# Linear attention into a GELU MLP on one core: batch 2's q in two halves round k, its v cast on GpSimd, and batch 3's k mapped at other blocks

## The chip, the cores and the metric

The kernel runs on one core of a Trainium2 chip. Time is device time in microseconds (us) for one execution. Before the change it is 272.56 us, the median of 6 runs (272.32 to 273.84).

## What is computed

A linear attention with the feature map elu + 1, over 8 batches of 8 heads, 576 positions and 64 values a head, and then a two-layer MLP with a tanh GELU over the 4608 tokens:

```
def phi(x):
    return np.where(x > 0, x, np.exp(x) - 1.0) + 1.0
q_p, k_p = (phi(q), phi(k))
kv = np.einsum('bhsd,bhse->bhde', k_p, v)
z = np.sum(k_p, axis=2)
num = np.einsum('bhsd,bhde->bhse', q_p, kv)
den = np.einsum('bhsd,bhd->bhs', q_p, z)[..., None] + 1e-06
x = (num / den)            # to (4608, 512)
h = x @ w_in               # 512 to 2048
g = 0.5 * h * (1.0 + np.tanh(c * (h + 0.044715 * h * h * h)))
return g @ w_out           # 2048 to 512
```

## The kernel before

The work goes in nine groups. Group j, for j from 0 to 7, takes 512 of the 576 positions of batch j; group 8 takes the 64 positions left over of each batch. For its group, PE (TensorE) makes 16 h blocks (`h_mm`, L391: four matmuls of 128x512 each, then a gelu on ACT at L406), and then the second layer, which from group 1 on is made by seven products (`Products`, L782) of quarters of g and w_out and of their sums and differences, a scheme that saves one product in eight. The sums of w_out are made once (`sum_w_out`, L744, four slices), those of g in each group (L755).

While PE works on group j, the attention of the next batches is prepared in between. The order is written out by hand: `at(j, slot, fn, ...)` registers a piece of work, and `iteration(j)` emits it after step `slot` of group j. In group 1 the steps 0 to 7 are the h blocks 0 to 7, 8 and 9 are products 1 and 7, 10 to 17 are the h blocks 8 to 15, and 18 to 22 are products 2, 6, 5, 4, 3. In groups 2 to 7 the steps 0 to 15 are h blocks, and the products follow. Each engine runs its own instructions strictly in the order in which they are emitted, and waits on semaphores for the others; pieces of one slot come in the order of their registration (`plan_third` first, then `plan_fourth`, and the sums of group 1 last).

For each batch there are these steps:

- q, k and v are loaded in fp32 by SP's DMA queue (L94 and L103) into a pool of seven buffers. Everything up to batch 4's k is issued at the start, as buffers come free.
- The map elu + 1 is the minimum of exp(x) and max(x + 1, 1): `exp_of` on ACT (L221), `linear_of` on DVE (L229) and `least_of` on DVE (L235). The result for k and q is `k_p` and `q_p`. ACT needs one table for exp and another for gelu; a change of table is an ACT_TABLE_LOAD (L419).
- `cast_v` brings v to bf16 (L240, tile `vp`, with a column of ones for the denominator).
- `kv_in_pair` multiplies k_p by vp on PE (L251) in a pair of PSUM banks that kv and n share, and DVE evicts the result (L678 for batch 2, L674 later).
- q_p is transposed by four DMA transposes on SP's queue, one for each of four chunks of 128 positions (`least_q`, L663, tile `qt`).
- n, for each chunk, multiplies qt by kv on PE (L267) and divides by the denominator on DVE (L284, L285, tile `xs`). The chunk is then transposed by SP's queue again into `xt` (L686), the right side of the next group's h blocks. From batch 3 on the n of all chunks is made at one place (L329).

Six PSUM banks of one pool serve the h blocks, the products and the n of some chunks. In group 1, products 1 and 7 keep two of them until the last products, which leaves four for the h blocks 8 to 15.

The change touches two hand-written plans, `plan_third` (batch 2, prepared during group 1) and `plan_fourth` (batch 3, prepared during groups 1 and 2), the helpers `exp_of`, `least_of` and `least_q`, and the slots of two sums in `iteration`. The tile `k_e`, which exp of k writes and `least_of` reads, exists once, so the exp of one batch's k waits for the k minimum of the batch before.

Of the kernel before, what the change touches and what calls it, by code (L numbers as in the profile page):

```python
# [9 lines left out]
BF16 = mybir.dt.bfloat16  # L10
# [6 lines left out]
def kernel(  # L17
# [16 lines left out]
    nc = tc.nc  # L34
# [3 lines left out]
    P = 128  # L38
    HP = P // 2
    C = 4  # L40
    MAIN = P * C
    REST = S - MAIN
    NP = H // 2
# [12 lines left out]
    pt = ctx.enter_context(tc.tile_pool(name="pt", bufs=2))  # L56
# [21 lines left out]
    def bank(name, shape, dt=FP32):  # L78
        return ps_b.tile(shape, dt, name=name, tag="b")
# [120 lines left out]
    def maps_view(name, b, x, out, hs):  # L200


        i = x[:, hs].rearrange("p h (c d) -> p h c d", d=D)
        o = out[:, :, hs, :].rearrange("p c h d -> p h c d")
        if name == "qr" or (name == "q" and b > 1):
            i = i.rearrange("p (u a) c d -> p a u c d", a=2)
            o = o.rearrange("p (a u) c d -> p a u c d", a=2)
        return o, i
# [2 lines left out]
        n, hn = ld[name, b].shape[2] // D, ld[name, b].shape[1]  # L211
        phi[name, b] = pphi.tile([P, n, hn, D], BF16, name=name + "_p")

    def exp_of(name, b, hs=None):
        x = ld[name, b]
        hs = hs or slice(0, x.shape[1])
        if (name, b) not in exps:
            e = name + ("_e" if name != "qr" or b % 2 else "_f")
            exps[name, b] = pe.tile([P, x.shape[2] // D, x.shape[1], D], BF16, name=e)
        o, i = maps_view(name, b, x, exps[name, b], hs)  # L220
        nc.scalar.activation(o, i, AF.Exp)  # L221

    def linear_of(name, b, hs=None):
# [4 lines left out]
        o, i = maps_view(name, b, x, phi[name, b], hs)  # L228
        nc.vector.tensor_scalar(o, i, 1.0, 1.0, op0=ALU.add, op1=ALU.max)  # L229

    def least_of(name, b, hs=None):
        p, e = phi[name, b], exps[name, b]
        if hs:
            p, e = p[:, :, hs, :], e[:, :, hs, :]
        nc.vector.tensor_tensor(p, p, e, op=ALU.min)  # L235


# [149 lines left out]
    xts, qts = {}, {}  # L387

    def h_mm(h_ps, xt, m, ts=slice(0, MAIN), blocks=range(KM)):
        for c in blocks:  # L390
            nc.tensor.matmul(  # L391
                h_ps[:, ts],
                lhsT=w_in_sb[:, c, P * m : P * (m + 1)],
                rhs=xt[:, c, ts],
                start=(c == 0),
                stop=(c == KM - 1),
                skip_group_check=True,
            )

    def gelu(j, g, m, h_ps):  # L400

        g_v, h_v = g[:, :, m, :], h_ps.rearrange("p (a n) -> p a n", a=2)
        if j == B:
            g_v = g[:, :, m, :].rearrange("p a (t n s) -> p (a t) s n", t=2, s=2)
            h_v = h_ps.rearrange("p (t s n) -> p t s n", t=C, s=2)
        nc.scalar.activation(g_v, h_v, AF.Gelu_apprx_tanh)  # L406
# [107 lines left out]
    def at(j, slot, fn, *args):  # L514


        fill.setdefault((j, slot), []).append((fn, args))

    def run(j, slot):
        for fn, args in fill.get((j, slot), ()):  # L520
            fn(*args)
# [70 lines left out]
    def plan_third():  # L592
        def n(c):
            transposed_x(2, c, (nab_in_banks if c == 3 else nab)(qts[2], 2, c))

        at(1, 1, sum_w_out, slice(0, 2))
        at(1, 2, linear_of, "k", 2)
        at(1, 3, linear_of, "q", 2)
        at(1, 4, cast_v, 2)
        at(1, 7, exp_of, "k", 2)  # L600
        at(1, 7, exp_of, "q", 2)
        at(1, 7, gelu_table)
        at(1, 9, least_of, "k", 2)
        at(1, 9, least_q, 2)
        at(1, 12, kv_in_pair, 2)
        for c, slot in enumerate((15, 17, 18, 18)):
            at(1, slot, n, c)

    def plan_fourth():

        at(1, 12, linear_of, "k", 3)
        at(1, 17, exp_of, "k", 3)
        at(1, 18, exp_of, "q", 3)
        at(1, 18, exp_of, "k", 4)
        at(1, 18, gelu_table)
        at(1, 21, linear_of, "q", 3)
        at(1, 22, least_of, "k", 3)
        at(2, 0, cast_v, 3)
        at(2, 0, least_q, 3)
        at(2, 4, kv_in_pair, 3)  # L620
        at(2, 5, linear_of, "k", 4)
        at(2, 5, least_of, "k", 4)
        at(2, 5, cast_v, 4)
        at(2, 8, linear_of, "q", 4)
        at(2, 15, exp_of, "q", 4)
        at(2, 16, exp_of, "k", 5)
        at(2, 19, least_q, 4)
        at(2, 22, linear_of, "k", 5)
        at(3, 0, least_of, "k", 5)
# [26 lines left out]
        at(j, 15, exp_of, "qr", m)  # L656
        at(j, 18, least)

    def least_q(b):
        least_of("q", b)  # L660
        qts[b] = pt.tile([P, C, NP, P], BF16, name="qt")
        for c in range(C):
            nc.sync.dma_start_transpose(  # L663
                out=qts[b][:, c],
                in_=phi["q", b][:, c].rearrange("p h d -> p (h d)"),
            )
# [16 lines left out]
    def transposed_x(b, c, x):  # L683
        if b not in xts:
            xts[b] = pt.tile([P, NP, MAIN], BF16, name="xt")
        nc.sync.dma_start_transpose(out=xt_chunk(b, c), in_=x)  # L686
# [16 lines left out]
    def finish(j, t, o_ps):  # L703
        if t % 2 == 0:
            o_sbs[j, t // 2] = pout.tile([P, 2, d_model], FP32, name="o_sb")
        o_sb = o_sbs[j, t // 2]
        if j == 0 and t in (1, 2):
            at(0, 35, evac, o_sb[:, t % 2, :], o_ps, True)
        else:
            evac(o_sb[:, t % 2, :], o_ps, t < C - 1 if j == 0 else t % 2)  # L710
        if t % 2 == 1:
            ov = out[j * S : j * S + MAIN, :].rearrange("(p c) f -> p c f", c=C)[:, t - 1 : t + 1]

            def store():
                nc.scalar.dma_start(out=ov, in_=o_sb)

            if j == 0:
                at(1, 2, store)
            else:
                store()  # L720

    def o_mm(o_ps, g, t, ms, half=None):
        for m in ms:
            if m == ms.start + 2 and half:
                run(*half)
            nc.tensor.matmul(  # L726
                o_ps,
                lhsT=g[:, t // 2, m, P * (t % 2) : P * (t % 2 + 1)],
                rhs=w_out_sb[:, :, m, :],
                start=(m == 0),  # L730
                stop=(m == MM - 1),
            )
# [139 lines left out]
    def iteration(j):  # L872
        xt = xts[j]
        if j < B:
            g = pg.tile([P, 2, MM, MAIN // 2], FP16, name="g")
        else:
            g = pg.tile([P, MM, 2, MAIN // 2], FP16, name="g").rearrange("p m a n -> p a m n")
        hs = [("h", m) for m in range(MM)]
        us = [range(m, m + 4) for m in range(0, MM, 4)]
        products = Products(j, g) if j else None  # L880
        early, late = slice(0, MM // 4), slice(MM // 4, MM // 2)
        if j == 0:
            us[2:3] = range(8, 10), range(10, 12)
            steps = hs + [("o", t, u) for u in us for t in range(C)]
        elif j == 1:
            steps = hs[:8] + [("product", n) for n in (1, 7)]
            steps += hs[8:] + [("product", n) for n in (2, 6, 5, 4, 3)]
            at(1, 7, products.third_sum, early, False)
            at(1, 7, products.third_sum, late, False)
            at(1, 7, sum_w_out, slice(2, 4))  # L890
            at(1, 13, products.sums, early)
            at(1, 17, products.sums, late)
            at(1, 19, products.last_sum)
        else:
            steps = [hs[i + n] for i in range(MM // 2) for n in (0, MM // 2)]
            steps += [("product", n) for n in (1, 5, 6, 7, 2, 4, 3)]
            for slot, ms in ((7, early), (15, late)):
                at(j, slot, products.sums, ms)
                at(j, slot, products.third_sum, ms)
            at(j, 16, products.last_sum)  # L900
        o_pss = {}
        for slot, step in enumerate(steps):
            if step[0] == "h":
                m = step[1]
                h_ps = h_begun.get(j, {}).get(m)
                if h_ps is None:
                    h_ps = bank("h_ps", [P, MAIN])
                    h_mm(h_ps, xt, m)
                gelu(j, g, m, h_ps)
            elif step[0] == "product":  # L910
                products.step(step[1])
            else:
                t, u = step[1:]
                if u.start == 0:
                    o_pss[t] = bank("o_ps", [P, d_model])
                o_mm(o_pss[t], g, t, u, half=(j, slot - 0.5))
                if u.stop == MM:
                    finish(j, t, o_pss[t])
            run(j, slot)

    plan_second()
    plan_third()
    plan_fourth()
    for j in range(3, 6):
        plan_prepare(j)
# [16 lines left out]
    for j in range(B + 1):  # L942
        iteration(j)
# [30 lines left out]
```

## Time and profile before

| what | value |
|---|---|
| median of 6 runs | 272.56 us |
| the profiled execution: whole time | 272.84 us |
| its span (first to last instruction) | 271.0 us |
| granted TensorE clock | 1.0 throughout |
| group 1's h block 8 begins | 57.93 us |
| group 2's first h block begins | 76.86 us |
| HBM read, written | 36.70 MB, 9.44 MB |

The profile is of one execution. A line of a timeline has start and duration in us, the engine, the line of the code, the operation, what it writes and reads, and the number of instructions merged; in square brackets the engine's idle time before it and what ended that. DVE is VectorE, ACT is ScalarE, POOL is GpSimd, and SPq is the queue of the sync engine, which only issues DMAs. A line of stretches has, for each engine, busy us and instructions, then the granted clock, the share of the DMA engines and GB/s. Matmuls overlap in the pipeline, so the duration of one (0.36 us) is more than the pace at which they start (0.216 us).

### The profile page before, as it was taken

What the parts mean: (1) busy time and instruction counts of PE and PEld (TensorE: products, weight loads), DVE (VectorE), ACT (ScalarE), POOL (GpSimd) and SP (SyncE); (2) the same over time, 40 slices, a digit from 0 to 9 for tenths busy, and PEclk for the clock granted to TensorE, in tenths of its full rate; (3) what the DMA queues carried; (4) which work ended last, traced back from release to release, by engine and by line L of the source; (5) the groups of instructions that cost most, each with busy time, mean ns of one, the idle gap of its engine ahead of it and who ended that gap; (6) DMA issues with size and microseconds to landing.
All of it is one profiled execution on the core that took longest, in us unless ns stands there. A gap on an engine that the chain in (4) does not pass through costs nothing.

```text
span 271.0 us, 5915 instructions
## 1 busy us (share of the span) xinstructions
PE 262.5 (97%) x2513; PEld 170.4 (63%) x2533; DVE 164.9 (61%) x263; ACT 165.7 (61%) x224; POOL 15.0 (6%) x21
## 2 busy tenths in 40 slices
PE   8899999998999999999999999999999999999994
PEld 3484455464854687558745874587458745874684
DVE  3860186987998966788738874683267316622262
ACT  4768878797939592669275926591765265028700
POOL 3047301000000000000000000000000000000000
PEclk9999999999999999999999999999999999999999
DMA  7999999997399996998698474216331412121004
GB/s 238 402 406 396 410 407 400 400 407 206 78 341 223 348 217 175 301 302 88 159 357 272 100 158 136 61 39 144 110 41 39 128 68 61 19 108 51 0 2 155
DMA packets 59786, 53.87 MB, mean 199 GB/s; under 512 B 35696, under 2 KB 45936, under 8 KB 59760
## 3 DMA queue, kind: packets, MB, share of 16 engines
q1 hardware_dynamic: 56880, 44.57, 57.3%
q10 hardware_dynamic: 2880, 8.91, 8.9%
q8 instruction: 20, 0.33, 0.5%
q14 instruction: 6, 0.05, 0.1%
HBM read 36.70 MB, written 9.44 MB: 170 GB/s over the span
## 4 chain that ended last, share of the span: by engine, by line
PE 90%; DMA 4%; ACT 2%; DVE 1%; SPq 1%; issue 1%
PE h_ps L391 43%; PE o_ps L782 36%; PE o_ps L726 5%; DMA v_x<-in_v_dram 3%; PE n_ps L329 1%; DMA qt<-q_p 1%; PE n_ps L251 1%; PE n_ps L267 1%; ACT k_e L221 1%; PE kv_ps L251 1%; PE t_ps L384 1%; SPq L94 1%; DVE k_p L235 1%; ACT L419 0%; SPq L99 0%
## 5 line engine op out<-in xcount | busy, mean ns | idle before, releaser
L391 PE MATMUL h_ps<-xt,w_in_sb 128*128 128x512 bf16 (+1 forms) x609 | 127.7, 361 | 1.1
L406 ACT ACTIVATE g<-h_ps 128x512 f16<-128x512 f32 x144 | 86.4, 620 | 58.6 <-PE h_ps L391 56.6
L391 PEld LDWEIGHTS <-w_in_sb 128*128 128x128 bf16 x628 | 58.1, 98 | 62.7 <-issue 0.7
L782 PEld LDWEIGHTS <-g 128*128 128x128 f16 x624 | 60.9, 98 | 9.0 <-ACT g L406 0.2
L782 PE MATMUL o_ps<-w_out_sb,g 128*128 128x256 f16 x496 | 58.2, 273 | 0.0
L854 DVE TENSOR_TENSOR o_sb<-o_ps,o_sb 128x512 f32<-128x512 f32 (+1 forms) x42 | 27.9, 666 | 29.6 <-PE o_ps L782 28.7
L755 DVE TENSOR_TENSOR s<-g 128x1024 f16<-128x1024 f16 x18 | 12.5, 692 | 39.6 <-ACT g L406 39.5
L782 PE MATMUL o_ps<-w_sum,s 128*128 128x256 f16 x256 | 29.3, 273 | 0.0
L782 PEld LDWEIGHTS <-s 128*128 128x128 f16 x272 | 26.6, 98 | 3.1
L285 DVE TENSOR_TENSOR xs<-n_ps,r 128x384 bf16<-128x384 f32 (+2 forms) x44 | 25.6, 582 | 1.5
L221 ACT ACTIVATE k_e<-k_x 128x2304 bf16<-128x2304 f32 (+1 forms) x9 | 17.2, 1914 | 6.0 <-DVE k_p L235 5.2
L826 ACT COPY o_sb<-o_ps 128x512 f32<-128x512 f32 x8 | 4.7, 585 | 22.2 <-PE o_ps L782 22.2
L229 DVE TENSOR_SCALAR q_p<-q_x 128x2048 bf16<-128x2048 f32 (+1 forms) x9 | 9.9, 1103 | 13.1 <-DMA q_x<-in_q_dram 13.1
L221 ACT ACTIVATE q_e<-q_x 128x2048 bf16<-128x2048 f32 (+1 forms) x9 | 15.5, 1721 | 2.8 <-DMA q_x<-in_q_dram 2.8
L782 PE MATMUL o_ps<-w_sum,g 128*128 128x256 f16 x128 | 15.3, 273 | 0.0
L726 PE MATMUL o_ps<-w_out_sb,g 128*128 128x512 f16 x64 | 15.1, 379 | 0.0
L229 DVE TENSOR_SCALAR k_p<-k_x 128x2304 bf16<-128x2304 f32 (+1 forms) x9 | 11.0, 1220 | 4.2 <-DMA k_x<-in_k_dram 4.2
L419 ACT ACT_TABLE_LOAD x9 | 11.5, 1283 | 0.2
L235 DVE TENSOR_TENSOR k_p<-k_p,k_e 128x2304 bf16<-128x2304 bf16 (+1 forms) x9 | 11.0, 1221 | 0.8 <-ACT k_e L221 0.4
L755 DVE TENSOR_TENSOR s<-s,g 128x1024 f16<-128x1024 f16 x16 | 11.1, 691 | 0.5
L240 DVE CAST vp<-v_x 128x2304 bf16<-128x2304 f32 (+1 forms) x9 | 11.0, 1225 | 0.5 <-DMA v_x<-in_v_dram 0.4
L235 DVE TENSOR_TENSOR q_p<-q_p,q_e 128x2048 bf16<-128x2048 bf16 (+1 forms) x9 | 9.9, 1102 | 0.9 <-ACT q_e L221 0.8
(63 smaller groups left out, 149.8 us busy)
## 6 DMA issues: line engine op xcount, KB each, us to landing
out_dram<-o_sb ACTq DMA_DIRECT2D x16, 512.0 KB, 4.2
k_x<-in_k_dram SPq DMA_DIRECT2D x7, 1152.0 KB, 11.5
v_x<-in_v_dram SPq DMA_DIRECT2D x7, 1152.0 KB, 12.2
q_x<-in_q_dram SPq DMA_DIRECT2D x6, 1024.0 KB, 11.0
w_st<-in_moe_w_in_dram SPq DMA_DIRECT2D x3, 1024.0 KB, 13.4
q_x<-in_q_dram SPq DMA_DIRECT2D x4, 512.0 KB, 8.5
w_st<-in_moe_w_out_dram SPq DMA_DIRECT2D x2, 1024.0 KB, 12.5
w_st<-in_moe_w_out_dram SPq DMA_DIRECT2D x4, 512.0 KB, 11.2
```

What stands on the lines that cost most here:

```text
L221: nc.scalar.activation(o, i, AF.Exp)
L229: nc.vector.tensor_scalar(o, i, 1.0, 1.0, op0=ALU.add, op1=ALU.max)
L235: nc.vector.tensor_tensor(p, p, e, op=ALU.min)
L240: fn(out=vp_paired(b)[:, :, us, 0:D].rearrange("p j u d -> p u j d"), in_=ld["v", b][:, us].rearrange("p u (j d) -> p u j d", d=D),)
L285: nc.vector.tensor_tensor(x_v, n_v[heads + (slice(0, D),)], r[heads + (None,)].to_broadcast(shape + [D]), op=ALU.mult,)
L391: nc.tensor.matmul(h_ps[:, ts], lhsT=w_in_sb[:, c, P * m : P * (m + 1)], rhs=xt[:, c, ts], start=(c == 0), stop=(c == KM - 1), skip_group_ ...
L406: nc.scalar.activation(g_v, h_v, AF.Gelu_apprx_tanh)
L419: nc.scalar.preload_act_table_set("gelu_apprx_tanh_and_others")
L726: nc.tensor.matmul(o_ps, lhsT=g[:, t // 2, m, P * (t % 2) : P * (t % 2 + 1)], rhs=w_out_sb[:, :, m, :], start=(m == 0), stop=(m == MM - 1),)
L755: nc.vector.tensor_tensor(out, i0, i1, op=op)
L782: nc.tensor.matmul(ps[t] if type(ps) is list else ps[:, t, :], lhsT=lhs[:, m, P * t : P * (t + 1)], rhs=rhs[:, m, :], start=(first and m = ...
L854: nc.vector.tensor_tensor(out, i0, i1, op=ALU.add)
```

## The change

In `plan_third` the exp of batch 2's q is split: the first two of its four chunks come before k's exp and the other two after it. Its minimum and its DMA transposes are split in the same way, the first half before k's minimum. The cast of its v moves from DVE to GpSimd, and in its place on DVE stands the third slice of `sum_w_out`. kv moves from slot 12 to 13 (one h block later), and the n of chunks 0 and 1 from slots 15 and 17 to 14 and 16 (one h block sooner). The first sums of g move from slot 13 to 14. In `plan_fourth`, batch 3's k has its linear part at slot 8 rather than 12 and its minimum at slot 20 rather than 22.

On the engines this gives, in group 1: DVE's order is k linear, q linear, third slice of w_sum, the two third sums, fourth slice, q minimum (first half), batch 3's k linear, k minimum, q minimum (second half), the two evictions of kv, the first n's division, and only then the first sums s0 and s1. Before, it was k linear, q linear, v cast, the two third sums, third and fourth slice, k minimum, q minimum, the evictions, batch 3's k linear, the first sums, the first n's division. On PE, kv has four h blocks (8 to 11) before it and one (12) between it and the first n; before, it was three and three. SP's order of DMAs is the same. GpSimd gets one instruction more, its last.

```
-    def exp_of(name, b, hs=None):
+    def exp_of(name, b, hs=None, cs=None):
...
         o, i = maps_view(name, b, x, exps[name, b], hs)
+        if cs:
+            o, i = o[..., cs, :], i[..., cs, :]
         nc.scalar.activation(o, i, AF.Exp)
...
-    def least_of(name, b, hs=None):
+    def least_of(name, b, hs=None, cs=None):
         p, e = phi[name, b], exps[name, b]
...
+        if cs:
+            p, e = p[:, cs], e[:, cs]
         nc.vector.tensor_tensor(p, p, e, op=ALU.min)
...
         at(1, 1, sum_w_out, slice(0, 2))
         at(1, 2, linear_of, "k", 2)
         at(1, 3, linear_of, "q", 2)
-        at(1, 4, cast_v, 2)
+        at(1, 4, sum_w_out, slice(2, 3))
+        at(1, 4, cast_v_paired, 2, slice(0, NP), nc.gpsimd.tensor_copy)
+        at(1, 7, exp_of, "q", 2, None, slice(0, 2))
         at(1, 7, exp_of, "k", 2)
-        at(1, 7, exp_of, "q", 2)
+        at(1, 7, exp_of, "q", 2, None, slice(2, C))
         at(1, 7, gelu_table)
+        at(1, 8, least_q, 2, slice(0, 2))
         at(1, 9, least_of, "k", 2)
-        at(1, 9, least_q, 2)
-        at(1, 12, kv_in_pair, 2)
-        for c, slot in enumerate((15, 17, 18, 18)):
+        at(1, 9, least_q, 2, slice(2, C))
+        at(1, 13, kv_in_pair, 2)
+        for c, slot in enumerate((14, 16, 18, 18)):
             at(1, slot, n, c)
...
-        at(1, 12, linear_of, "k", 3)
+        at(1, 8, linear_of, "k", 3)
         at(1, 17, exp_of, "k", 3)
         at(1, 18, exp_of, "q", 3)
         at(1, 18, exp_of, "k", 4)
         at(1, 18, gelu_table)
+        at(1, 20, least_of, "k", 3)
         at(1, 21, linear_of, "q", 3)
-        at(1, 22, least_of, "k", 3)
...
-    def least_q(b):
-        least_of("q", b)
-        qts[b] = pt.tile([P, C, NP, P], BF16, name="qt")
-        for c in range(C):
+    def least_q(b, cs=slice(0, C)):
+        least_of("q", b, cs=cs)
+        if b not in qts:
+            qts[b] = pt.tile([P, C, NP, P], BF16, name="qt")
+        for c in range(cs.start, cs.stop):
             nc.sync.dma_start_transpose(
...
-            at(1, 7, sum_w_out, slice(2, 4))
-            at(1, 13, products.sums, early)
+            at(1, 7, sum_w_out, slice(3, 4))
+            at(1, 14, products.sums, early)
             at(1, 17, products.sums, late)
```

## The prediction

> **What bounds the kernel now.** I read the page's first part, then PE's timeline around its only long wait, then the chain of waits through the changed blocks, and last the sync engine's issues with their times to landing.
>
> ```profile
> span 271.0 us, 5915 instructions
> PE 262.5 (97%) x2513; PEld 170.4 (63%) x2533; DVE 164.9 (61%) x263; ACT 165.7 (61%) x224; POOL 15.0 (6%) x21
> 57.93 2.75 PE L391 MATMUL h_ps<-xt,w_in_sb 128*128 128x512 bf16 x11
> 60.61 0.78 PE L251 MATMUL kv_ps<-vp,k_p 64*64 64x65 bf16 x72
> 61.32 2.90 PE L391 MATMUL h_ps<-xt,w_in_sb 128*128 128x512 bf16 x11
> 65.39 0.41 PE L267 MATMUL n_ps<-kvbd,qt 128*128 128x130 bf16 x4 [1.17 <-DMA qt<-q_p]
> 61.70 3.64 DMA qt<-q_p
> 77.66 1.36 DVE k_p L235
> 79.05 2.13 ACT k_e L221
> 81.19 1.28 ACT L419
> 82.48 0.61 ACT g L406
> 83.13 6.20 PE h_ps L391 x28
> ```
>
> Lines of the timeline and of the chain begin with start and duration in us. PE is the bound, so the change can win only where PE stands still: at two places. At 65.39 the first n of batch 2 waits for its transposed q. Six h blocks precede it, three before kv and three after; the last of them began its last matmul at 63.85, a matmul's pace is 0.216, so PE was free at 64.07 and lost 1.32. At 83.13 an h block of group 2 waits for a PSUM bank that group 2's first gelu (82.48 + 0.60) frees; the block before it began its last matmul at 82.63, so 82.85 was due and 0.28 was lost. That gelu was late through batch 3's k minimum on DVE (77.66), the exp of batch 4's k and the table load. More than 1.60 us is not to be had.
>
> The chain charges the first wait to the transpose from its issue at 61.70, released by DVE's q minimum (60.41 + 1.23). Whether an earlier q helps depends on what lies ahead of it in SP's queue (the last number of an issue line is us to landing; of a window line, GB/s):
>
> ```profile
> 48.79 1.95 SPq L94 DMA_DIRECT2D k_x<-in_k_dram  x1
> k_x<-in_k_dram SPq DMA_DIRECT2D x1, 1152.0 KB, 15.9
> ...
> k_x<-in_k_dram SPq DMA_DIRECT2D x1, 1152.0 KB, 17.1
> ...
> 88.03 0.53 SPq L94 DMA_DIRECT2D v_x<-in_v_dram  x1
> v_x<-in_v_dram SPq DMA_DIRECT2D x1, 1152.0 KB, 12.2
> ...
> 91.21 2.63 SPq L686 DMA_TRANSPOSE xt<-xs  x1
> xt<-xs SPq DMA_TRANSPOSE x1, 9.6
> ...
> 58.00:61.80 3.80, 3.69 (x86) 1.92 (x87) 3.00 (x4) 3.77 (x4) 0.00 (x0) 1.00 1.04 406
> 62.60:64.20 1.60, 1.60 (x8) 0.53 (x6) 1.60 (x2) 1.60 (x5) 0.00 (x0) 1.00 1.06 192
> ```
>
> Batch 4's k, issued at 48.79, lands at 64.69; batch 3's k, issued at 42.09, at 59.2. The xt transpose issued at 91.21 took 9.6, where the page's median is 2.4: it landed at 100.8, just behind the v load (88.03 + 12.2 = 100.2) issued ahead of it. A transpose on this queue waits for the loads in front of it. Batch 2's first transpose landed at 61.70 + 3.64 = 65.34, that is 0.65 behind batch 4's k, and the engines run at full rate (406 GB/s) until about 62.6. So it was probably the load, and not q, that came last, and an issue 3.5 earlier gains little.
>
> **The change, part by part.**
>
> *q in halves round k.* ACT now does half of q (1.06 by the 128x1024 row), k (2.13) and the other half (1.06) where it did k and q (2.13 + 1.91): 0.2 more, before a table load after which PE's banks have slack (four are free; the first gelu moves from 61.69 to about 61.9, its bank is asked for at 62.6). The first half's exp ends at 56.45 + 1.06 = 57.51; DVE's half minimum (0.69) ends at 58.2. SP has nothing between batch 4's k and these transposes, so two of the four are issued at 58.2 rather than 61.70; the others follow the second half at about 62.5, long before their n (after 69.5).
>
> *Batch 3's k linear.* It moves on DVE from behind kv's eviction to between q's first half and k's minimum. It needs a load that lands at 59.2; DVE stands from 58.2 to 59.24, then linear 1.27 (pace between starts), k minimum to 61.86. Behind it wait k's minimum, q's second half and kv's eviction. PE reaches kv after four h blocks at 57.93 + 3.46 + 0.09 = 61.48 and now waits until 61.9, kv ends 62.6, the two evictions (0.86) at 63.5; the one h block left between kv and n ends at 63.5 too. So n is ready for PE at 63.55 apart from q: this costs nothing while q lands later, and 0.4 if q came early.
>
> *n one block sooner.* PE is asked for the first n after five h blocks, not six. If q lands at the same time, one h block (4 x 0.216 = 0.865) that used to fill the wait is left to do after it. This is the main cost. The sums of s0 and s1 now come after the first n's division; the second half of them ends near 70.2, the product that reads it starts near 70.9. w_sum's third slice takes the place of the v cast on DVE (1.23 for 1.36).
>
> *v cast on GpSimd.* The row for 2048 elements is 1.90, so 2304 take 2.14. Its load landed at 50.5 and kv needs it at 61.9, but DVE is busy:
>
> ```profile
> 14.43 1.04 POOL L140 CAST w_in_sb<-w_st 128x1024 bf16<-128x1024 f32 x1 [0.24 <-DMA w_st<-in_moe_w_in_dram]
> 18.34 1.56 POOL L140 CAST w_in_sb<-w_st 128x1024 bf16<-128x1024 f32 x1 [2.86 <-DMA w_st<-in_moe_w_in_dram]
> 18.31 0.69 DVE L140 CAST w_in_sb<-w_st 128x1024 bf16<-128x1024 f32 x1 [0.95 <-DMA w_st<-in_moe_w_in_dram]
> ```
>
> The same cast took 0.52 longer beside a DVE cast, which itself was not slowed (0.69 is its lone row too). From 50.5 on DVE idles about 0.5 before 57.5 and 1.0 at 58.2 to 59.2, with short gaps between instructions besides, so I expect the cast done by 59 to 62.8. Bounds: no cost at all; or, if GpSimd held DVE off for its 2.14, the s0 sums and product 7 would be late by 1.1 (56.18 to 57.3), n ready at 64.3: still ahead of q. Both hidden by q's landing; I take nothing. The cover ends if the cast ends after 63.4 (63.4 + 0.71 + 1.1 = 65.2).
>
> The Trainium skill's SBUF — State Buffer, section on its two separate sides, says that GpSimd and such DVE instructions lock a port pair for a whole instruction and the loser blocks. The row shows GpSimd as the loser; by the rule DVE can lose too, up to 2.14, and the sum stays the same for the reason just given.
>
> *Batch 3's k minimum at block 20.* It runs near 75.7 instead of 77.66 even with everything 0.5 later; the exp of batch 4's k, the table load and the first gelu follow at about 80.5 instead of 82.48, and the 0.28 goes. Behind it two additions of output and q's linear are 0.8 later, but the bank they free is next asked for after five h blocks.
>
> *Sum.* With q's first quarter landing at t, n starts at t + 0.05 against 65.39, with 0.865 more to do after and 0.28 less: t + 0.05 - 65.39 + 0.865 - 0.28 = t - 64.75. The descriptors now wait ready behind the load, so I take t a little under the old 65.34: 65.2, a loss of 0.45. Ends: with the load's engines all done by 62.9 (half rate after 62.6), 62.9 + 0.65 = 63.55 (gain 1.2); with a delay like that of the second xt transpose, issued at 93.97 and landing 8.9 later, 2.7 behind the load, 67.4 (loss 2.65). The old row lies nearest, being the same transpose behind the same load: 64.4 to 66.0, or -0.35 to +1.25, is this case's own range. The profiled execution's 272.84 (span 271.0 and 1.84 around it) becomes 273.29; it lies 0.28 over the median of the runs, 272.56, which becomes 273.0 (own range 272.2 to 273.8).
>
> **Rivals.**
> - *The transposes overtake the load.* For it: the old first one had packets moving before the load landed. Against: the 9.6 of xt. Then kv's wait and eviction set n at 63.55, a gain of 1.2: 271.4, or 271.9 if GpSimd holds DVE.
> - *GpSimd is kept off until DVE waits for it.* If DVE's short gaps are of no use and the cast gets in only at 62.4, after q's second half, it ends at 64.55, kv at 65.3, its eviction at 66.35 and n at 66.4: 1.0 + 0.865 - 0.28 = 1.6 slower, 274.1. It decides once the cast ends after 63.4. Against: the idle 1.0 at 58.2.
> - *The sooner k minimum saves nothing*, because the additions behind it hold the banks: 0.28 more, 273.3.
>
> **How the numbers follow.** A difference under about 0.3% (0.8 us) can't be told from none here. The first case has 0.57 (0.45 within that bound, 0.12 above it), the overtaking 0.18, the shut-out cast 0.18, the last 0.07 (0.04 and 0.03). So faster 0.18, the same 0.49, slower 0.33. The range, 271.6 to 274.2, takes in most of both outer cases, and leaves some 0.07 below and 0.1 above.
>
> **What would show it.** Right: two q transposes issued near 58 and landing with or just behind batch 4's k, near 65; PE's wait before the first n about 1.7 after a short one before kv; DVE idle before k's linear until about 59.2; no wait at group 2's sixth h block. Wrong: a landing well before batch 4's k, or a GpSimd cast that ends after 63.4, or PE waiting anywhere after 70.

## The result, and the profile after

The changed kernel takes 273.17 us (median of 20 runs, 273.04 to 273.61) against 272.60 us for the kernel before on the same chips (40 runs, 272.32 to 275.55). By the medians it is 0.57 slower, and each of its 20 runs is slower than 31 of the 40 of the kernel before. The ratio, which is taken over all the runs and not from the medians, is 1.0011 with a 95% interval of 0.9998 to 1.0023; it shows no difference, because nine runs of the kernel before (273.69 to 275.55) lie above all the rest and raise its mean. The prediction was 273.0. The profiled execution took 273.18 us, 0.34 more than the one before, which lies 0.28 over its own median (272.56); the traces can account only for the 0.34.

The page's first part, of the kernel after:

```profile
span 271.3 us, 5922 instructions
PE 262.6 (97%) x2513; PEld 170.2 (63%) x2533; DVE 165.2 (61%) x263; ACT 166.4 (61%) x225; POOL 18.4 (7%) x22
```

POOL has its one instruction more (21 to 22) and 3.4 us more of busy time. PE's timeline through the changed blocks (start, duration, and in brackets the idle time before and what ended it; the lines of the code that are shown now stand 2 to 8 further down):

```profile
56.92 2.09 PE L790 MATMUL o_ps<-w_out_sb,s 128*128 128x256 f16 x16 [0.59 <-DVE s L763]
58.84 3.62 PE L395 MATMUL h_ps<-xt,w_in_sb 128*128 128x512 bf16 x15
...
64.99 0.41 PE L271 MATMUL n_ps<-kvbd,qt 128*128 128x130 bf16 x4 [0.86 <-DMA qt<-q_p]
...
77.36 4.48 PE L395 MATMUL h_ps<-xt,w_in_sb 128*128 128x512 bf16 x19
81.77 0.91 PE L255 MATMUL kv_ps<-vp,k_p 64*64 64x65 bf16 x72
...
89.62 0.67 PE L333 MATMUL n_ps<-kv,qt 64*128 64x65 bf16 x32
```

The lines of before at the same places, where the prediction does not show them:

```profile
56.18 1.91 PE L782 MATMUL o_ps<-w_out_sb,s 128*128 128x256 f16 x16
76.86 4.48 PE L391 MATMUL h_ps<-xt,w_in_sb 128*128 128x512 bf16 x19
89.27 0.67 PE L329 MATMUL n_ps<-kv,qt 64*128 64x65 bf16 x32
```

Milestone by milestone:

| PE reaches | before | after | difference |
|---|---|---|---|
| h block 8 of group 1 | 57.93 | 58.84 | +0.91 |
| first n of batch 2 | 65.39 | 64.99 | -0.40 |
| group 2's first h block | 76.86 | 77.36 | +0.50 |
| group 2's n of the rest | 89.27 | 89.62 | +0.35 |
| the end (span) | 271.0 | 271.3 | +0.3 |

So the first n does start 0.40 sooner. From it to group 2 there is 0.90 more to do (77.36 - 64.99 = 12.37 against 11.47): the h block that no longer fills the wait, four matmuls of 0.216. In group 2, 0.15 comes back, and nothing changes after that. A new wait of 0.59 stands before product 7, at 56.92; before, product 7 began at 56.18 without one.

The timelines of POOL and of DVE show where that wait comes from:

```profile
50.69 3.36 POOL L244 CAST vp<-v_x 128x2304 bf16<-128x2304 f32 x1 [7.99 <-DMA v_x<-in_v_dram]
```

```profile
50.70 1.35 DVE L231 TENSOR_SCALAR k_p<-k_x 128x2304 bf16<-128x2304 f32 x1
51.97 3.17 DVE L231 TENSOR_SCALAR q_p<-q_x 128x2048 bf16<-128x2048 f32 x1
...
58.52 0.68 DVE L239 TENSOR_TENSOR q_p<-q_p,q_e 128x1024 bf16<-128x1024 bf16 x1
59.25 1.36 DVE L231 TENSOR_SCALAR k_p<-k_x 128x2304 bf16<-128x2304 f32 x1
```

The cast alone was estimated at 2.14, from the row for 2048 elements. It starts beside DVE's k linear (1.35, as long as ever), ends at 54.05, and so took 1.2 more. DVE's q linear, 1.22 without a GpSimd instruction beside it, stands at 3.17: it is held for 1.95, until the cast has ended. The sums that product 7 reads are late by that much less DVE's slack, and so is q's first minimum, which starts at 58.52.

Last, the chain of waits of the kernel after (start, duration, what). Ahead of these lines it goes from DVE's q linear through the third slice of w_sum and the sums to product 7:

```profile
59.26 5.68 DMA qt<-q_p
...
64.99 0.41 PE n_ps L271 x4
```

The first transpose is issued 2.44 sooner than before (59.26 for 61.70), takes 2.04 longer, and lands at 64.95. Batch 4's k, ahead of it in SP's queue, lands at 64.37 here.

### The profile page after: what moved, and what is told of

Read it like the earlier page. It is cut to its first block, busy times and chain, and to the rows that moved or that the text cites. A ratio compares the mean times of both kernels' runs of the same rounds, so it can differ in the third digit from the quotient of the medians.

```text
span 271.3 us, 5922 instructions
## 1 busy us (share of the span) xinstructions
PE 262.6 (97%) x2513; PEld 170.2 (63%) x2533; DVE 165.2 (61%) x263; ACT 166.4 (61%) x225; POOL 18.4 (7%) x22
## 4 chain that ended last, share of the span: by engine, by line
PE 88%; DMA 5%; DVE 4%; SPq 1%; issue 1%; ACT 0%; DVEq 0%
PE h_ps L395 42%; PE o_ps L790 36%; PE o_ps L734 5%; DMA v_x<-in_v_dram 3%; DMA qt<-q_p 2%; PE n_ps L333 1%; DVE q_p L231 1%; PE n_ps L255 1%; PE n_ps L271 1%; DVE w_sum L752 1%; PE kv_ps L255 1%; PE t_ps L388 1%; SPq L94 1%; DVE k_p L231 0%; DVE w_out_sb L752 0%
## 5 line engine op out<-in xcount | busy, mean ns | idle before, releaser
L231 DVE TENSOR_SCALAR q_p<-q_x 128x2048 bf16<-128x2048 f32 (+1 forms) x9 | 11.9, 1318 | 13.1 <-DMA q_x<-in_q_dram 13.1
```

## The experiments

Each is one edit of the kernel after or of the kernel before; times are medians of 12 runs, with the range, and ratios, again over all runs, are to the kernel before on the same chip (its medians there: 272.63 in experiments 1 to 4, 272.55 in 5 to 8, 272.57 in 9 and 10).

**1. n back at its old blocks (`n_as_before`; the kernel after with this edit).**

```
-        for c, slot in enumerate((14, 16, 18, 18)):
+        for c, slot in enumerate((15, 17, 18, 18)):
```

> The changed kernel with the n of chunks 0 and 1 back at blocks 15 and 17. Theory (batch 4's k load holds the transposes, the sooner n only takes one h block out of the wait): the first quarter of q still lands near 65.0, PE comes to n near 64.8 with six h blocks done and hardly waits, and the time falls by about 0.7 us against the changed kernel, to about 272.4 us, level with or 0.2 under before. Rival (q's earliness decides, n's place is free): within 0.2 us of the changed kernel's 273.2.

Measured: 272.17 us (272.03 to 272.47), ratio 0.9951 (0.992 to 0.9982). PE's timeline there:

```profile
65.01 0.41 PE L271 MATMUL n_ps<-kvbd,qt 128*128 128x130 bf16 x4
```

The n starts at the same 65.0, now behind another h block and with hardly an idle time (0.2 by the pace). Moving n one block sooner therefore costs 1.0 us, and the rest of the change taken together gains 0.46 by the medians. Of the 1.0, 0.13 is batch 3's kv in group 2, which takes 0.78 here again: it took 0.91 in the three traces of the kernel after that keep n at the earlier blocks (the kernel after itself and experiments 2 and 3), and 0.78 in all others.

**2. v cast on DVE again (`v_on_dve`; the kernel after with this edit).**

```
-        at(1, 4, cast_v_paired, 2, slice(0, NP), nc.gpsimd.tensor_copy)
+        at(1, 4, cast_v_paired, 2, slice(0, NP), nc.vector.tensor_copy)
```

> The changed kernel with batch 2's v cast by VectorE at the place where GpSimd's instruction stands. Theory: q's linear on VectorE goes from 3.2 back to 1.2 us and product 7's wait of 0.75 us goes, but the wait before the first n grows by as much, as q lands with batch 4's k near 65; the time stays within 0.2 us of 273.2. Rival (the held VectorE costs what product 7 waits): 272.4 us.

Measured: 273.31 us (273.12 to 273.51), ratio 1.0008 (0.9982 to 1.0035). DVE's timeline, then PE's:

```profile
52.02 1.22 DVE L231 TENSOR_SCALAR q_p<-q_x 128x2048 bf16<-128x2048 f32 x1
...
59.34 1.36 DVE L231 TENSOR_SCALAR k_p<-k_x 128x2304 bf16<-128x2304 f32 x1 [0.76 <-DMA k_x<-in_k_dram]
```

```profile
62.03 0.78 PE L255 MATMUL kv_ps<-vp,k_p 64*64 64x65 bf16 x72 [0.19 <-DVE k_p L239]
...
65.12 0.41 PE L271 MATMUL n_ps<-kvbd,qt 128*128 128x130 bf16 x4 [1.35 <-DMA qt<-q_p]
```

Everything that the GpSimd cast had pushed moves back, q's linear to 1.22 and product 7 to 56.30 without a wait; the wait returns as 1.35 before the first n. It is the same idle time at another place: what sets the first n, in both, is the transpose behind the load. In this trace the first transpose was issued at 58.65, 0.61 sooner than in the kernel after, and landed 0.13 later, at 65.08, as batch 4's k did (64.50 for 64.37).

**3. Batch 4's k load behind q's first half (`load_after_q_half`; the kernel after with this edit).**

```
         load_all_pairs("k", k, b)
         load_all_pairs("v", v, b)
-    load_all_pairs("k", k, 4)
...
         at(1, 8, least_q, 2, slice(0, 2))
+        at(1, 8, load_all_pairs, "k", k, 4)
```

> The changed kernel with batch 4's k load issued behind the first two q transposes. Theory: the first quarter lands just behind batch 3's v (61.5), near 62; n then waits only for kv and its eviction and starts near 64.1, so 0.8 to 0.9 us under the changed kernel: about 272.3 us. Rival (transposes do not wait for loads ahead of them): landing as before near 65 or later, no gain, 273.2 us.

Measured: 273.75 us (273.6 to 276.29), ratio 1.0024 (0.9992 to 1.0055). The first part came as expected: the first transpose landed 2.9 after its issue at 59.29, not 5.68, at 62.15, which is 0.60 behind batch 3's v (61.55), the load that now stood ahead of it, and n began at 64.27. The expected gain did not come. In the same trace, PE's timeline and the chain of waits:

```profile
70.11 0.89 PE L270 MATMUL n_ps<-kvbd,qt 128*128 128x130 bf16 x8 [0.78 <-DMA qt<-q_p]
```

```profile
63.87 6.69 DMA qt<-q_p
```

The load, issued at 61.99, now stands ahead of q's second half. Its last transpose, issued at 63.87, took 6.69 and landed at 70.56, 1.06 after the load; group 2 begins at 77.83 instead of 77.36. The mechanism is the same, one half later: this confirms that a transpose lands behind the load ahead of it, and the edit costs more than it gains.

**4. The kernel before with batch 4's k load behind all four transposes (`before_load_after_q`).**

```
-    load_all_pairs("k", k, 4)
...
         at(1, 9, least_q, 2)
+        at(1, 9, load_all_pairs, "k", k, 4)
```

> The kernel before with one line moved: batch 4's k load issued behind batch 2's four q transposes, nothing else. Theory: the first transpose, issued at 61.7, lands about 2.4 us later at 64.1, PE's wait of 1.3 us before the first n shrinks to about 0.1, and the time falls by 1.2 us to about 271.35 us; batch 4's k, landing near 70, is not asked for until 79. Rival (the chain's reading: q's minimum at 61.64 is what is late): 0 to 0.3 us gain.

Measured: 272.25 us (271.83 to 272.4), ratio 0.9963 (0.9938 to 0.9988): a gain (all 12 runs lie under all 35 of the kernel before there), but by the medians, 0.38, a third of the one expected; the profiled execution's span is 0.7 shorter. PE's timeline:

```profile
64.68 0.41 PE L266 MATMUL n_ps<-kvbd,qt 128*128 128x130 bf16 x4 [0.48 <-DMA qt<-q_p]
```

The first transpose landed 2.95 after its issue, where 2.4 had been expected, and 0.48 of the wait is left. It took 1.86 to issue; the other three took 1.25 to 1.27. A 16 KB fetch of instructions, 1.04 long, occupied one DMA engine from about 62.0 on, just behind that issue; whether it is the cause was not tried. The load now stands ahead of the four transposes of xt instead: the first three take 5.1 to landing by the median, where in the kernel after it is 2.3. That cost nothing here, but the margin is small: the last of the four lands near 75.5, and group 2, which reads them, begins at 76.15.

**5. n as before and the load behind all of q, GpSimd's cast kept (`load_last_gpsimd`; the kernel after with this edit).**

```
-    load_all_pairs("k", k, 4)
...
         at(1, 9, least_q, 2, slice(2, C))
+        at(1, 9, load_all_pairs, "k", k, 4)
...
-        for c, slot in enumerate((14, 16, 18, 18)):
+        for c, slot in enumerate((15, 17, 18, 18)):
```

> The changed kernel with n back at blocks 15 and 17 and batch 4's k load issued behind all four q transposes; v is still cast by GpSimd. Theory: q no longer sets n (first quarter near 62.2, the last near 66, before the load), but PE comes to n only at 64.8 because product 7 waited for the VectorE that GpSimd held, so against the run with n alone put back (272.17 us) only its last 0.2 us of waiting goes: 272.0 us. Rival (the load alone was the trouble): near 271.2 us.

Measured: 271.96 us (271.82 to 272.13), ratio 0.9956 (0.9932 to 0.9981). PE's timeline:

```profile
57.05 2.09 PE L790 MATMUL o_ps<-w_out_sb,s 128*128 128x256 f16 x16 [0.59 <-DVE s L763]
...
64.97 0.40 PE L270 MATMUL n_ps<-kvbd,qt 128*128 128x130 bf16 x4
```

With the load out of the way, PE's only idle time left in group 1 is the 0.59 before product 7, that is, DVE held by GpSimd: what that hold had cost unseen is now on the path.

**6. The same with the cast on DVE behind q's first half, and batch 3's k linear at slot 15 (`load_last_dve`; experiment 5 with this edit).**

```
-        at(1, 4, cast_v_paired, 2, slice(0, NP), nc.gpsimd.tensor_copy)
...
         at(1, 8, least_q, 2, slice(0, 2))
+        at(1, 8, cast_v, 2)
...
-        at(1, 8, linear_of, "k", 3)
+        at(1, 15, linear_of, "k", 3)
```

> As load_last_gpsimd, with v cast by VectorE behind q's first half and batch 3's k linear at block 15, behind kv. Theory: with q out of the way the hold of VectorE has its price, and taking it away gives about 0.8 us: no wait at product 7, before kv, before n or at group 2's sixth block, PE at the first n by 64.1 us, time 271.2 us. Rival (the hold is hidden by something else still): within 0.2 us of load_last_gpsimd.

Measured: 272.11 us (272.01 to 272.29), ratio 0.997 (0.995 to 0.999). This is the rival's case, within 0.2 of experiment 5. PE reached the first n at 64.11, 0.86 sooner as expected, and gave it all back before group 2 (76.46 for 76.44). The chain of waits shows how:

```profile
63.84 0.70 DVE s L763
...
65.53 0.69 DVE xs L288
66.22 1.26 DVE k_p L230
...
69.71 3.23 PE o_ps L790 x28
```

DVE works in its order: sums that wait for a gelu until 63.82, then the division of the first n, whose matmuls had been done since 64.5, then batch 3's k linear, the second division, and only then the sums that product 6 needs at 69.71. An earlier n is of no use while its division stands behind something later.

**7. n one block sooner in the kernel before (`n_sooner_alone`; the edit of experiment 1, the other way).**

> The kernel before with only the n of chunks 0 and 1 moved to blocks 14 and 16. Theory: q's first quarter still lands near 65.3, so the one h block taken out of the wait (4 x 0.216 = 0.865 us) is paid in full: 272.6 + 0.86 = 273.45 us, with a wait of about 2.2 us before the first n. Rival (the place of n is free while q is late): 272.6 us.

Measured: 274.79 us (273.31 to 276.66), ratio 1.0076 (1.0043 to 1.0109). The runs fall into three groups: four from 273.31 to 273.56, as expected; three from 274.71 to 274.85; and five from 275.72 to 276.66, the profiled one among them. Its PE timeline, and then the stretches in and behind the wait (busy us and instructions of PE, its weight loads, DVE, ACT and POOL, then the clock, the DMA share and GB/s):

```profile
66.65 0.41 PE L267 MATMUL n_ps<-kvbd,qt 128*128 128x130 bf16 x4 [3.33 <-DMA qt<-q_p]
66.89 2.72 PE L391 MATMUL h_ps<-xt,w_in_sb 128*128 128x512 bf16 x8
```

```profile
63.30:66.60 3.30, 0.02 (x1) 0.00 (x0) 1.83 (x3) 1.39 (x3) 0.00 (x0) 1.00 0.88 89
66.90:71.20 4.30, 4.30 (x19) 1.91 (x17) 1.80 (x4) 1.19 (x2) 0.00 (x0) 0.60 0.36 80
```

In this execution the transpose landed at 66.60, 1.26 later than in the profile of before. The load ahead of it had landed at 64.46, no later than there (64.67), so the load does not explain that. The wait grew to 3.33, and after it the granted clock was 0.60 on the mean of 4.3 us (in finer stretches 0.50 from 68.0 to 71.2): eight h matmuls took 2.72 instead of 1.89. From 71.4 on it was 1.0 again. A clock of 0.60 for 4.3 us loses 1.7. The two sizes fit the groups: 273.45 + 1.26 = 274.7, and 1.7 more is 276.4; the five have a mean clock of 0.994, the others of 0.999 or 1.0. Why the transpose lands late in some executions is open. In this one a 16 KB fetch of instructions, 1.2 long, occupied one DMA engine from about 64.4 on, and from 65.6 to 66.3 packets came only one at a time; whether it is the cause was not tried.

The kernel before shows the same two sizes in some of its own runs: of its 35 on this chip, four lie between 273.72 and 274.05 with a clock of 0.998 to 1.0, and three between 275.39 and 275.66 with 0.992 to 0.994. In the five experiments with the load behind all four transposes (4, 5, 6, 9 and 10), none of the 60 runs is so late.

**8. Batch 3's k minimum sooner in the kernel before (`k_min_sooner_alone`).**

```
+        at(1, 20, least_of, "k", 3)
         at(1, 21, linear_of, "q", 3)
...
-        at(1, 22, least_of, "k", 3)
```

> The kernel before with only batch 3's k minimum moved from block 22 to 20. Theory: the wait of 0.28 us at group 2's sixth h block goes and nothing else changes: 272.3 us. Rival (the additions behind the minimum hold the banks instead): 272.6 us or a little more.

Measured: 272.38 us (272.06 to 273.65), ratio 0.9977 (0.9949 to 1.0005); by the runs alone nothing is decided. PE's timeline is clearer:

```profile
76.75 4.48 PE L391 MATMUL h_ps<-xt,w_in_sb 128*128 128x512 bf16 x20
...
88.88 0.66 PE L329 MATMUL n_ps<-kv,qt 64*128 64x65 bf16 x32
```

From group 2's first h block to its n it is 12.13, where before it was 89.27 - 76.86 = 12.41. The wait at the sixth block is gone, and with it 0.28.

**9. DVE's order mended (`sums_after_n`; experiment 6 with this edit).**

```
-        at(1, 15, linear_of, "k", 3)
+        at(1, 9, linear_of, "k", 3)
...
-            at(1, 14, products.sums, early)
+            at(1, 15, products.sums, early)
```

> The kernel of load_last_dve (n at slots 15 and 17, batch 4's k load behind all four q transposes, v cast on DVE behind q's first half), with batch 3's k linear moved to DVE's idle stretch between q's second half and kv's eviction (61.45 to 62.4 there) and the first sums s0 and s1 behind the first n's division. Theory: load_last_dve gave its 0.85 us back through DVE's order alone: the division of n0 stood behind sums that waited for a gelu, and product 6's sums stood behind batch 3's k linear. Then n0 stays at 64.1, n1 and product 6 follow without their waits of 0.3 and 0.34, group 2's first h block begins near 75.7 instead of 76.46, and the median is near 271.4 us. Rival: the bank wait of 0.17 behind the late gelus and the late exp set the pace, whatever DVE's order is: then some other wait appears before group 2 and the median stays at 272.0 to 272.2. A third: the linear overruns the idle stretch (1.27 in 0.95) and pushes kv's eviction so that n0 itself waits: n0 at 64.3 or later.

Measured: 271.47 us (271.38 to 271.64), ratio 0.9955 (0.9936 to 0.9973). PE's timeline:

```profile
62.39 1.89 PE L394 MATMUL h_ps<-xt,w_in_sb 128*128 128x512 bf16 x7 [0.17 <-ACT g L409]
64.12 0.40 PE L270 MATMUL n_ps<-kvbd,qt 128*128 128x130 bf16 x4
...
75.78 2.54 PE L394 MATMUL h_ps<-xt,w_in_sb 128*128 128x512 bf16 x10
```

The first n stays at 64.1, product 6 follows its predecessor without a wait, and group 2 begins at 75.78, 1.08 before the kernel before and 1.58 before the kernel after, and of PE's waits only the 0.17 for a bank is left. This is the best version of the study: 1.1 us (0.4%) faster than before, and 1.7 us faster than the kernel after. Which of the two moves does how much was not tried.

**10. The two simplest gains in the kernel before (`before_two_moves`: the edits of experiments 4 and 8).**

> The kernel before with two edits only: batch 4's k load behind the four q transposes of batch 2, and batch 3's k minimum at slot 20 instead of 22. Theory: the two gains are of separate waits and add up: 0.38 by the medians of before_load_after_q and 0.17 by k_min_sooner_alone (0.64 and 0.28 by their waits), so 272.0 us by the medians, 271.7 by the waits, the wait at group 2's sixth h block is gone and n0 begins near 64.7. Rival: the first gain was noise, or the instruction fetch at 62.0 varies: then 272.3.

Measured: 272.3 us (271.78 to 272.59), ratio 0.9975 (0.9949 to 1.0). The profiled execution, at 271.8 with n at 64.72 and no wait at the sixth block, is what the sum of the two waits gives, but it is one of the fastest of the twelve. The medians do not add up, and what differs between the executions was not seen, since each kernel has one trace.

## Why the prediction was right

The predicted 273.0 lies 0.17 under the median, and its sum, t - 64.75 with t the landing of the first quarter of q, holds with the trace's own t: 64.95 gives +0.20, and 0.13 more comes from batch 3's kv, which took 0.91 instead of 0.78; together 0.33 against the 0.34 between the two profiles. Why that kv was slower was not tried. That the predicted time lies so close is in part luck: the prediction had a loss of 0.45, the profiles give 0.34, and the medians 0.57.

- *Where PE stood still* (1.32 before the first n, 0.28 at group 2's sixth block): right. Experiment 9 removed nearly all of it, and its span is 1.4 shorter, 269.6 for 271.0.
- *q behind batch 4's k*: right. Experiment 3 shows it from both sides: a transpose issued at the same 59.3 lands 2.9 after its issue without batch 4's k ahead and 5.68 after it with that load, and when the load is put ahead of the second half, that half lands late instead. Nine traces agree. In each a load was still on its way when the first transpose was issued, at some time between 58.26 and 61.70, and the transpose landed 0.56 to 0.67 behind it: behind batch 4's k (64.37 to 64.67) in the kernels before and after and in experiments 1, 2 and 8, behind batch 3's v (61.55 to 61.64) in experiments 3, 5, 6 and 9. The exception is experiment 7, with 2.14. The term was mis-sized by 0.25: I took t = 65.2, it was 64.95, since the load landed 0.30 sooner than before (64.37 for 64.67) and the waiting transpose 0.58 after it. The load's issue had not moved (48.79, 48.82), so that 0.30 may belong to the execution and not to the change; no run separates the two. The first issue came at 59.26 and not near 58, which changed nothing. The Trainium skill (DMA: Bandwidth & Descriptors, section on queues, rings and completion order) says that each DMA engine consumes the descriptors of one issuer's ring in order; the rows of experiment 3 agree. The rival in which the transposes overtake falls with this.
- *n one block sooner costs 0.865*: right. The stretch from n to group 2 grew by 0.90, and experiment 1 got 1.0 back, kv's 0.13 included.
- *v cast on GpSimd, priced at nothing*: right in the sum, wrong in the mechanism. I expected GpSimd to be the loser, with the cast done by 59 to 62.8, from a row in which GpSimd's cast took 0.52 longer and DVE's was not slowed. In fact each was held for nearly the whole of the other's instruction: GpSimd 1.2 beside DVE's k linear, then DVE 1.95 beside the cast, which was done at 54.05. The Trainium skill (SBUF — State Buffer, section on its two separate sides), on which the prediction draws, allows for this: the engine that comes second is blocked for the whole instruction of the first. The trace agrees, with 1.95 for a cast estimated at 2.14. The case that I had set as a bound came, at a smaller size: product 7 began at 56.92, 0.74 late where the bound was 1.1, hidden by q's landing. Experiment 2 shows it hidden (273.31 without the hold); experiment 5 shows it in the open, once the load no longer covers it. Its price alone was not isolated: experiment 9, 0.49 faster than experiment 5, changes DVE's order as well. The rival in which GpSimd is shut out falls too.
- *Batch 3's k linear and kv*: the signature was wrong. I expected DVE to stand until 59.24 and PE to wait briefly before kv. In the kernel after, DVE had been held so long by then that it reached the linear at 59.25, when the load had just landed; in experiment 2, without the hold, both waits are there, 0.76 on DVE and 0.19 before kv. PE's waits before product 7 and before n, 0.75 and 1.02 by the pace of its matmuls, together make the 1.7 that I had put before n alone.
- *Batch 3's k minimum saves 0.28*: right, by experiment 8. In the kernel after its minimum ran at 75.39 instead of 77.66 and the wait at the sixth block was gone. The rival in which it saves nothing falls.

The change's gain thus went three ways. An earlier q bought at most 0.40, because the queue and not q set its landing, and by the medians less (0.46 for everything but the move of n, of which the k minimum's wait is 0.28); moving n up gave away 0.9 of work that had filled the wait; and GpSimd's help held back the engine that it was to relieve. Experiments 5, 6 and 9 together say that the load had covered two later limits: GpSimd's hold on DVE, and DVE's order of sums and division. What the split of q alone is worth was not tried.

## What to carry to other kernels

When a transfer is late, look first at what stands ahead of it in its queue and when that lands; issuing sooner behind a long load moves little (0.61 sooner and no earlier landing, in experiment 2), while putting the load behind the small transfers moved their landing from 65.0 to 62.2 here, provided that all of them are ahead of it, and provided that what is issued behind the moved load can wait. Filling work should stay in front of a wait until the wait is really gone. And when a wait is removed, ask in which order the next engine will take its work, since each limit here covered the next: the load, then GpSimd's hold on DVE, then DVE's order.

## What was not expected of the hardware

- GpSimd and DVE holding each other: one GpSimd cast, estimated at 2.14 alone, stretched DVE's linear from 1.22 to 3.17, and was itself stretched to 3.36. In the four traces with this cast on GpSimd that linear took 3.16 to 3.17, and in the other eight 1.22.
- An idle time of PE of 3.33 us was followed by 4.3 us at a mean granted clock of 0.60, 0.50 for the most of it, so that a wait cost half as much again as it lasted; the wait of 1.17 in the profile of before was followed by none (clock 1.0). The Trainium skill (TensorE: Matmul & The Clock Gate, section on what is actually happening) names an idle window of about 3.4 us after which the clock is halved. The row of experiment 7 agrees with it, in a kernel whose PE hardly stands still otherwise.
